# The last two output tiles of the second network's weights: prepared in the first chunk's expansion, from a staging pool

## The chip, the cores and the metric

One NeuronCore of a Trainium2 chip runs the whole program; the other cores are idle. The metric is the device time of one execution in microseconds (us). The engines are called PE (TensorE, matmuls), PEld (its weight loads), ACT (ScalarE), DVE (VectorE), POOL (GpSimd) and SP (SyncE, which here issues nearly all DMAs). Each engine works through its own list of instructions in a fixed order; an instruction that waits holds all that stand behind it on its engine.

## What is computed

Attention over 2304 tokens of width 512 (4 batches, 8 heads), then two feed-forward networks, one behind the other, all in float32:

```python
x = attention(q_l, k_l, v_l, q_g, k_g, v_g)            # 2304 x 512
g = x @ moe_w_gate                                     # first network, 512 -> 1536
x = (g * sigmoid(g) * (x @ moe_w_val)) @ moe_w_out     # 1536 -> 512
h = x @ moe2_w_in                                      # second network, 512 -> 2048
y = (max(h, 0) + alpha * min(h, 0)) @ moe2_w_out       # 2048 -> 512
```

The change touches only the weights `moe2_w_in` and `moe2_w_out` of the second network: when and from which memory they are prepared. What is computed stays the same.

## The kernel before

**Precision.** The weights arrive as 64-bit words. A float32 is taken out of each by ACT and DVE (`convert_steps`: ACT L765 and L766, DVE L768, L771, L777), and then split in a high and a low part (`split`: ACT copies the high half, L853, DVE subtracts for the low half in two pieces, L856). A product of two split operands is three matmuls. Blocks are multiplied by a scheme of Winograd's kind, seven products in place of eight, for which sums of weight blocks are wanted too: `block_sums` (L865) and `column_sums` (four DVE steps, L875).

**The second network's weights.** The generator `w2_prepare` does this for 16 tiles of 128 x 1024 words: for i = 0..3 the tiles ("x", 2i), ("x", 2i+1) of `w_in` and ("o", i), ("o", i+4) of `w_out`. A tile is loaded to a buffer `dbl` of 1 MB (L882), converted into `raw`, summed, split back into `dbl` and stored to DRAM (L890, 1 MB a store) as one of the arrays `w2sx`, `w2ss`, `w2so`, `w2st13`, `w2st42`. An "x" tile gives two stores, an "o" tile with j < 4 one, an "o" tile with j >= 4 three: its own, and with the tile j-4 the two sums t13 and t42. The `yield`s cut it into small steps, which the caller advances with `next(w2gen)` between its own instructions. The tile for the next item is loaded ahead.

**Stages.** Attention and two visits of the first network run under a planner; behind it (`nc.flush()`) comes the third visit of the first network, a loop over j = 0..5 of products (matmul L1278) and of the contraction `down3` (matmul L1335), in which `next(w2gen)` is called once or twice after each product and whose last turn, j = 5, begins by draining the generator. From there on the order on each engine is set when the program is built, by a list scheduler that goes by data dependences, buffers and the order of writing.

**The second network** runs over three chunks c of tokens. The expansion `up(c, jp)`, jp = 0..3, goes through seven products b11, t1, t2, b21, t3, b22, t4, each for jj = 0, 1, six matmuls each (L1483) into the banks ps_g and ps_v, ps_a, or ps_acc. ACT copies some partial sums out (L1514: `p` for b11 and t1, `u` for t2); t2 adds to the bank of b11 and t3 to that of t2. DVE adds the copies (L1508), ACT takes the two halves of the leaky relu (`hst`, L1500; `neg`, L1501) and DVE joins them (L1502) in `hst`. Then the contraction `down(c)` multiplies `hst` by `w_out` (also L1483, 256 columns). Its operands are tiles `as`, a ring of three, hi by ACT (L1581) and lo by DVE (L1582), after subtractions (L1561) for some products. The first two steps of the contraction are written inside jp = 3 already.

**Fetches.** `fetch_up` brings 1 MB for two products into one of four slots (four DMAs of 256 KB, L1253), `fetch_down` brings 1 MB of `w_out` weights into a ring of three (two DMAs, L1368); `down3` calls it for the first three at j = 3, 4, 5. All stand in SP's one list. The memory of `two` (the pool of `hst`, the temporary tiles and the `as` ring) is taken on the right side of SBUF before chunk 0 begins.

## Time and profile before

| | us |
|---|---|
| median of 3 runs | 870.16 (869.02 to 870.22) |
| profiled execution | 872.43 |
| its span in the trace | 870.6 |

The profile's page gives PE as busy for 850.0 us (98% of the span), PEld for 767.0, DVE for 655.3 and ACT for 568.8. The share of PE is above 0.9 in nearly all of the 40 slices. The span is what the trace covers; the execution's time lies 1.8 us above it. On the trace's clock the third visit of the first network runs from about 399 to 522 us, chunk 0's expansion from 522 to 586.4 (jp 1 begins at 542.7, jp 2 at 557.25, jp 3 at 571.8), and its contraction follows. A row's "idle before <-releaser" says how long the engine stood before the instruction, and what ended that.

### The profile page before, as it was taken

The numbers are of one execution on the slowest core, as the hardware profiler recorded it, in microseconds if no ns is written. First come the engines' busy times: TensorE is split into PE (matmuls) and PEld (weight loads), VectorE is DVE, ScalarE is ACT, GpSimd is POOL, SyncE is SP. The second block draws the span as 40 slices with busy tenths as digits, with TensorE's granted clock in tenths as the row PEclk, the third lists the DMA queues.
The fourth block names the chain that finished last, engine by engine and source line by source line (L and its number), as shares of the span: only waits on it lengthen the run. The fifth ranks groups of instructions, "written<-read, shape, count | busy, mean of one in ns | idle before, by whom it ended". The sixth has DMA issues, their size and how long they took to land.

```text
span 870.6 us, 18942 instructions
## 1 busy us (share of the span) xinstructions
PE 850.0 (98%) x7570; PEld 767.0 (88%) x7570; DVE 655.3 (75%) x1333; ACT 568.8 (65%) x1111; POOL 0.7 (0%) x6
## 2 busy tenths in 40 slices
PE   6899999999999999999999999999999999999997
PEld 5677778788788787888999999999999999999997
DVE  3987999988697665779989885589727699536863
ACT  4989999877567586655534446685437765357643
POOL 0000000000000000000000000000000000000000
PEclk9999999999999999999999999999999999999999
DMA  9799989899976869987898869887788887799497
GB/s 345 290 397 409 372 328 390 320 375 371 405 263 228 343 220 349 376 327 293 287 329 326 298 214 291 254 256 245 247 290 283 251 256 244 249 348 294 150 307 237
DMA packets 124312, 262.48 MB, mean 302 GB/s; under 512 B 7872, under 2 KB 96576, under 8 KB 109888
## 3 DMA queue, kind: packets, MB, share of 16 engines
q1 hardware_dynamic: 124224, 261.27, 85.0%
q8 instruction: 60, 0.98, 0.4%
q14 instruction: 28, 0.23, 0.1%
HBM read 198.06 MB, written 63.18 MB: 300 GB/s over the span
## 4 chain that ended last, share of the span: by engine, by line
PE 79%; ACT 7%; DVE 6%; DMA 5%; issue 2%; SPq 0%; ACTq 0%; DVEq 0%
PE ps_acc L1483 17%; PE ps_a L1483 10%; PE acc L274 9%; PE v L274 8%; PE g L274 8%; PE ps_g L1483 5%; PE a L274 5%; PE ps_v L1483 4%; PE ps_v L1278 3%; PE ps_g L1278 3%; PE ps_acc L1335 3%; PE ps_a L1335 2%; ACT e L274 2%; ACT L274 1%; DMA yp<-in_w_dram 1%
## 5 line engine op out<-in xcount | busy, mean ns | idle before, releaser
L1581 ACT ACTIVATE as<-hst 128x768 fp32r<-128x768 f32 (+2 forms) x100 | 70.3, 716 | 67.4 <-PE ps_acc L1483 41.8
L274 PE MATMUL g<-xa,w 128*128 128x512 f32 x432 | 107.7, 397 | 0.7 <-DVE xa L274 0.3
L1483 PE MATMUL ps_acc<-w,as 128*128 128x256 f32 x864 | 107.2, 282 | 0.7 <-DMA w<-w2st 0.4
L274 PE MATMUL v<-xa,w 128*128 128x512 f32 x432 | 107.1, 397 | 0.0
L274 PE MATMUL acc<-h,w 128*128 128x512 f32 x432 | 106.4, 395 | 0.5 <-DVE h L274 0.4
L1483 PEld LDWEIGHTS ps_acc<-w,as 128*128 128x128 f32 x864 | 104.6, 188 | 1.1 <-issue 0.5
L1582 DVE TENSOR_TENSOR as<-hst,as 128x768 fp32r<-128x768 f32 (+2 forms) x100 | 78.2, 793 | 34.4 <-ACT as L1581 34.0
L274 PEld LDWEIGHTS g<-xa,w 128*128 128x128 f32 x432 | 79.0, 188 | 20.5 <-issue 1.8
L274 PEld LDWEIGHTS acc<-h,w 128*128 128x128 f32 x432 | 79.7, 188 | 19.5 <-issue 1.4
L274 PEld LDWEIGHTS v<-xa,w 128*128 128x128 f32 x432 | 79.3, 188 | 18.4 <-issue 1.4
L274 ACT ACTIVATE e<-e,mx 128x128 f32<-128x128 f32 (+1 forms) x136 | 57.2, 423 | 19.3 <-DVE mx L274 18.9
L274 ACT ACT_TABLE_LOAD x42 | 53.9, 1283 | 10.3 <-PE g L274 8.9
L1502 DVE SCALAR_TENSOR_TENSOR hst<-neg,nal,hst 128x384 f32<-128x384 f32 (+1 forms) x96 | 56.5, 594 | 4.4 <-ACT neg L1501 2.6
L1483 PE MATMUL ps_a<-w,as 128*128 128x256 f32 x384 | 47.7, 281 | 0.0
L1483 PEld LDWEIGHTS ps_a<-w,as 128*128 128x128 f32 x384 | 46.5, 188 | 0.0
L1508 DVE TENSOR_TENSOR p<-ps_acc,p 128x384 f32<-128x384 f32 (+1 forms) x24 | 12.7, 531 | 43.6 <-PE ps_acc L1483 43.6
L274 DVE TENSOR_TENSOR t<-v,sg 128x512 f32<-128x512 f32 x36 | 24.7, 685 | 19.9 <-PE a L274 11.2
L1500 ACT ACTIVATE hst<-p 128x384 f32<-128x384 f32 (+1 forms) x48 | 24.3, 506 | 17.1 <-DVE p L1508 15.0
L274 PE MATMUL a<-qk 64*32 64x128 f32 (+1 forms) x1072 | 28.6, 294 | 5.4 <-DMA qk<-in_qk_dram 2.5
L1409 ACT ACTIVATE hring<-t 128x320 fp32r<-128x320 f32 x24 | 11.2, 467 | 32.3 <-DVE t L1408 32.3
L274 PEld LDWEIGHTS a<-qk 64*32 64x32 f32 x1072 | 18.9, 109 | 14.6 <-issue 4.0
L274 ACT ACTIVATE raw<-dbl 128x1024 f32<-128x1024 f32 x24 | 27.6, 1152 | 6.4 <-DMA w2ss<-raw 4.5
(265 smaller groups left out, 1740.8 us busy)
## 6 DMA issues: line engine op xcount, KB each, us to landing
dbl<-in_w_dram SPq DMA_DIRECT2D x28, 1024.0 KB, 8.6
w<-w2ss SPq DMA_DIRECT2D x96, 256.0 KB, 4.6
w<-w2st SPq DMA_DIRECT2D x48, 512.0 KB, 5.3
w<-w2so SPq DMA_DIRECT2D x40, 512.0 KB, 5.5
w<-w2sx SPq DMA_DIRECT2D x72, 256.0 KB, 4.7
v<-in_v_dram SPq DMA_DIRECT2D x15, 1024.0 KB, 9.8
qk<-in_qk_dram SPq DMA_DIRECT2D x14, 688.0 KB, 9.9
w2sx<-dbl SPq DMA_DIRECT2D x8, 1024.0 KB, 8.2
```

The costliest lines, as they stand in the source:

```text
L274: last[o.eng] = getattr(getattr(self.nc, o.eng), o.op)(*o.args, **o.kw)
L1278: nc.tensor.matmul(out=o[:, 0:n], lhsT=left(name, a, k), rhs=x[name][:, b, k, 0:n], start=(i == 0), stop=(i == 5),)
L1335: mm = nc.tensor.matmul(out=o, lhsT=a, rhs=x, start=(first and e == 0 and not second), stop=((j, f, e) == (NF1 // 2 - 1, 0, 2) and i not i ...
L1409: nc.scalar.activation(out=hi, in_=t, func=ACTF.Copy)
L1483: pe["last"] = nc.tensor.matmul(skip_group_check=True, **k)
L1500: nc.scalar.activation(out=h, in_=u, func=ACTF.Relu)
L1502: nc.vector.scalar_tensor_tensor(out=h, in0=g, scalar=nal[:, i:i + 1], in1=h, op0=ALU.mult, op1=ALU.add)
L1508: nc.vector.tensor_tensor(out=u, in0=o[:, 0:n], in1=u, op=ALU.add)
L1581: nc.scalar.activation(out=d[:, 0], in_=s, func=ACTF.Copy)
L1582: nc.vector.tensor_tensor(out=d[:, 1], in0=s, in1=d[:, 0], op=ALU.subtract)
```

## The change

`w2_prepare` is given the list of its tiles, the functions that give it buffers, and a number `pause`. The old generator does all but the last two tiles, ("o", 3) and ("o", 7). A second one, `w2rest`, does these two in chunk 0's expansion, from a pool `stage` on the right side: one `dbl` buffer of 8 KB per partition, and two `raw` buffers of 4 KB. With `pause` = 8 it waits eight calls before the conversion of each tile and before each of the two sums, and loads the second tile only after the first is stored. It is advanced once after each product and jj for jp < 3 and drained after the last product of jp = 2; then `stage` is released, and the operand ring `as` is allocated in its place as a pool `asp`, instead of in `two`. `fetch_down(1)` and `fetch_down(2)` move there too.

```diff
--- before.py
+++ after.py
@@ -875,7 +875,9 @@
             nc.vector.tensor_tensor(out=o, in0=x, in1=y, op=ALU.subtract)
             yield
 
-    def w2_prepare():
+    W2_ORDER = [(z, j) for i in range(NJ // 2) for z, j in (("x", 2 * i), ("x", 2 * i + 1), ("o", i), ("o", i + NJ // 2))]
+
+    def w2_prepare(todo, dbl_tile, raw_tile, pause):
 
         def land(z, j):
             dbl = dbl_tile()
@@ -897,13 +899,11 @@
             nc.sync.dma_start(out=w2s[key][:, 1], in_=raw)
             st["tail"] = False
 
-        todo = []
-        for j in range(NJ // 2):
-            todo += [("x", 2 * j), ("x", 2 * j + 1), ("o", j), ("o", j + NJ // 2)]
         dbl = land(*todo[0])
         for n, (z, j) in enumerate(todo):
-            ahead = land(*todo[n + 1]) if n + 1 < len(todo) else None
-            yield
+            ahead = land(*todo[n + 1]) if n + 1 < len(todo) and not pause else None
+            for _ in range(max(pause, 1)):
+                yield
             raw = raw_tile()
             yield from convert_steps(dbl, raw)
             yield
@@ -920,8 +920,10 @@
             else:
                 yield from column_sums(upper, raw)
                 for key, t in (("t13", upper), ("t42", raw)):
+                    for _ in range(pause):
+                        yield
                     yield from out_to((key, j - NJ // 2), t)
-            dbl = ahead
+            dbl = land(*todo[n + 1]) if pause and n + 1 < len(todo) else ahead
 
     def passes(a, b):
         return ((a[0], b[0]), (a[0], b[1]), (a[1], b[0]))
@@ -1101,7 +1103,7 @@
         att_tags["list"] = ["a0", "a1"]
         att_tags["i"] = 0
 
-        w2gen = w2_prepare()
+        w2gen = w2_prepare(W2_ORDER[:-2], dbl_tile, raw_tile, 0)
 
         def pumper(nslots, target, wrate=1.0, g=1.0):
             k0 = st["k"]
@@ -1344,7 +1346,8 @@
                 want_w1(2 * j + 6, "o")
                 wload(True)
             else:
-                fetch_down(j + 3 - NF1 // 2)
+                if j == 3:
+                    fetch_down(0)
 
         DOWN = (("b11", "b11"), ("s1", "t1"), ("s2", "t2"), ("a12", "b21"), ("s3", "t3"), ("s4", "b22"), ("a22", "t4"))
         HOME = {"b11": ("o", 0, 0), "b12": ("o", 0, 1), "b21": ("o", 4, 0), "b22": ("o", 4, 1),
@@ -1471,7 +1474,18 @@
 
             return hst[:, kt:kt + n, half(c) * q:half(c) * q + half(c)]
 
-        tags = {}
+        stage = tc.alloc_tile_pool(name="stage", bufs=1, side="right", reuse_waits="tile")
+        staged = {}
+
+        def stage_tile(size, dtype):
+            def new():
+                n = staged[size] = staged.get(size, 0) + 1
+                tag = "stage%d_%d" % (size, n % (1 if size == 2048 else 2))
+                return stage.tile([128, size * 4 // mybir.dt.size(dtype)], dtype, tag=tag, name="stage", bufs=1)
+
+            return new
+
+        w2rest = w2_prepare(W2_ORDER[-2:], stage_tile(2048, I64), stage_tile(1024, F32), 8)
 
         def temp(tag):
             return two.tile([128, 2, NT], F32, tag=tag, name=tag, bufs=1)
@@ -1567,7 +1581,7 @@
 
         def operand(c, what, kt):
 
-            t = two.tile([128, 2, 2, NT], F32R, tag="as%d" % (st["as"] % 3), name="as", bufs=1)
+            t = ring["as"].tile([128, 2, 2, NT], F32R, tag="as%d" % (st["as"] % 3), name="as", bufs=1)
             st["as"] += 1
             n = 256 if c == 2 else NT
             srcs = []
@@ -1735,6 +1749,15 @@
                     if jp == 3 and jj == 1 and name in ("b22", "t4"):
                         next(steps)()
                     tasks()
+                    if c == 0 and jp < NJ // 2 - 1:
+                        next(w2rest, None)
+                    if c == 0 and (jp, name, jj) == (NJ // 2 - 2, "t4", 1):
+                        for _ in w2rest:
+                            pass
+                        stage.release()
+                        ring["as"] = tc.alloc_tile_pool(name="asp", bufs=1, side="right", reuse_waits="tile")
+                        fetch_down(1)
+                        fetch_down(2)
             while late:
                 late.popleft()()
             extra.extendleft(reversed(list(s1_work(c, 3))))
@@ -1742,6 +1765,7 @@
                 pass
             while extra:
                 extra.popleft()()
+        ring["as"].release()
         two.release()
         slope.release()
         edge.release()
```

In the changed kernel the line numbers are shifted: L884 load and L892 store of the preparation, L1514, L1515, L1516 the relu (before L1500 to L1502), L1528 the copies (L1514), L1595 and L1596 the operand tiles (L1581, L1582).

The list scheduler moves instructions, in three places above all. The first is ACT around the end of jp 1 and the start of jp 2. In the kernel before (`hst` and `neg` are the relu's halves, `p` the copies that jp 2's first products leave):

```order
L1501 ACTIVATE neg<-p_6013 128x384 [waits Activation_49]
L1500 ACTIVATE hst<-u_6034 128x384 [waits DVE_49]
L1501 ACTIVATE neg<-u_6034 128x384 [waits Activation_49]
L1500 ACTIVATE hst<-u_6034 128x384 [waits DVE_49]
L1501 ACTIVATE neg<-u_6034 128x384 [waits Activation_49]
L1500 ACTIVATE hst<-ps_acc_5985 128x384 [waits PE_49]
L1501 ACTIVATE neg<-ps_acc_5985 128x384 [waits DVE_49]
L1500 ACTIVATE hst<-ps_acc_5998 128x384 [waits PE_49]
L1501 ACTIVATE neg<-ps_acc_5998 128x384 [waits DVE_49]
L1581 ACTIVATE as<-hst 128x768 [waits DVE_49]
L1514 ACTIVATE p_6144<-ps_g 128x384 [waits PE_49]
L1514 ACTIVATE p_6144<-ps_v 128x384 [waits PE_49]
```

The changed kernel at the same place:

```order
L1514 ACTIVATE hst<-p_5979 128x384 [waits DVE_49]
L1515 ACTIVATE neg<-p_5979 128x384 [waits Activation_49]
L1514 ACTIVATE hst<-u_6004 128x384 [waits DVE_49]
L765 ACTIVATE stage<-stage 128x1024 [waits DMAHW1_49]
L766 ACTIVATE stage<-stage 128x1024 [waits DMAHW4_49]
L1515 ACTIVATE neg<-u_6004 128x384 [waits Activation_49]
L1514 ACTIVATE hst<-u_6004 128x384 [waits DVE_49]
L1515 ACTIVATE neg<-u_6004 128x384 [waits Activation_49]
L1514 ACTIVATE hst<-ps_acc_5948 128x384 [waits PE_49]
L1515 ACTIVATE neg<-ps_acc_5948 128x384 [waits DVE_49]
L1528 ACTIVATE p_6120<-ps_g 128x384 [waits PE_49]
L1514 ACTIVATE hst<-ps_acc_5963 128x384
```

The two steps of tile ("o", 7)'s conversion stand between the halves of one relu, with a wait for its load; the operand tile is gone from here.

The second place is ACT where the expansion ends. Before, the list reads (two other `as` tiles stand earlier still, at the start of jp 1):

```order
L1500 ACTIVATE hst<-ps_acc_6294 128x384 [waits PE_49]
L1501 ACTIVATE neg<-ps_acc_6294 128x384 [waits DVE_49]
L1500 ACTIVATE hst<-ps_acc_6307 128x384 [waits PE_49]
L1501 ACTIVATE neg<-ps_acc_6307 128x384 [waits DVE_49]
L1031 ACTIVATE xa<-yp_94 128x2x128
L1581 ACTIVATE as<-hst 128x768 [waits PE_49] x3
```

In the changed kernel, where these are the first tiles `as` of all:

```order
L1514 ACTIVATE hst<-ps_acc_6301 128x384 [waits PE_49]
L1515 ACTIVATE neg<-ps_acc_6301 128x384 [waits DVE_49]
L1514 ACTIVATE hst<-ps_acc_6314 128x384 [waits PE_49]
L1515 ACTIVATE neg<-ps_acc_6314 128x384 [waits DVE_49]
L1595 ACTIVATE as<-hst 128x768 [waits DMAHW1_49]
L1595 ACTIVATE as<-hst 128x768 x2
```

All of the first three operand tiles have moved behind the last relu of jp 3, and the first waits for a DMA, the last store out of `stage`. Earlier in the same jp 3 ACT has the split for that store:

```order
L1514 ACTIVATE hst<-p_6308 128x384 [waits DVE_49]
L1515 ACTIVATE neg<-p_6308 128x384 [waits Activation_49]
L853 ACTIVATE stage<-stage 128x1024 [waits DMAHW3_49,Activation_49]
L1514 ACTIVATE hst<-p_6308 128x384 [waits DVE_49]
L1515 ACTIVATE neg<-p_6308 128x384 [waits Activation_49]
```

It stands between two relu pairs and waits for the store of t13 (`w2st_3` out of the same buffer). On SP the two last stores stand so, among the fetches for chunk 1 (`w2sx_165` and on; `DMAHW` and a number are the DMA queues' counters):

```order
L1255 DMA w<-w2sx_4890 128x2x256 [waits DMAHW2_49]
L892 DMA w2st_3_6281<-stage 128x2048 [waits DMAHW3_49,DVE_49,Activation_49]
L1371 DMA w<-w2so_5961 128x4x256 [waits DMAHW4_49]
L1255 DMA w<-w2sx_165 128x2x256 [waits DMAHW5_49,PE_49]
L1255 DMA w<-w2sx_170 128x2x256 [waits DMAHW6_49]
L1255 DMA w<-w2ss_166 128x2x256 [waits DMAHW7_49]
L1255 DMA w<-w2ss_171 128x2x256 [waits DMAHW0_49]
L892 DMA w2st_3_6286<-stage 128x2048 [waits DMAHW1_49,DVE_49,Activation_49]
L1255 DMA w<-w2ss_166 128x2x256 [waits DMAHW2_49,PE_49]
```

Where before only fetches stood:

```order
L1253 DMA w<-w2ss_4656 128x2x256 [waits DMAHW2_49,PE_49]
L1253 DMA w<-w2ss_5029 128x2x256 [waits DMAHW3_49]
L1253 DMA w<-w2sx_4495 128x2x256 [waits DMAHW4_49]
L1253 DMA w<-w2sx_4892 128x2x256 [waits DMAHW5_49]
L1253 DMA w<-w2sx_165 128x2x256 [waits DMAHW6_49,PE_49]
L1253 DMA w<-w2sx_170 128x2x256 [waits DMAHW7_49]
L1253 DMA w<-w2ss_166 128x2x256 [waits DMAHW0_49]
L1253 DMA w<-w2ss_171 128x2x256 [waits DMAHW1_49]
L1253 DMA w<-w2ss_166 128x2x256 [waits DMAHW2_49,PE_49]
```

The two stores are new in this place; each waits for ACT's and DVE's halves of its split, and the fetches behind it wait with it.

## Rows read from the trace of the kernel before

**Rows 1.** Windows: start:end length, busy us per engine (instructions), PE clock, DMA share, GB/s
```profile
424.00:446.00 22.00, 20.64 (x138) 20.22 (x137) 20.04 (x43) 12.26 (x20) 0.00 (x0) 1.00 0.89 305
446.00:500.00 54.00, 53.99 (x367) 53.64 (x366) 46.41 (x96) 23.21 (x40) 0.00 (x0) 1.00 0.89 324
500.00:522.20 22.20, 22.20 (x155) 21.91 (x154) 17.91 (x37) 10.38 (x20) 0.00 (x0) 1.00 0.66 208
522.20:542.70 20.50, 20.50 (x123) 20.13 (x123) 11.96 (x27) 11.75 (x33) 0.00 (x0) 1.00 0.93 293
...
571.80:586.40 14.60, 14.60 (x87) 14.60 (x86) 12.11 (x22) 11.19 (x27) 0.00 (x0) 1.00 0.84 260
```

**Rows 2.** Waits of PE from 424 to 586: us in total, times, longest
```profile
PE ps_v L1278 <- ACT p L1294: 1.4, 1, 1.4
```

**Rows 3.** Timeline of ACT at 441: start, us, instruction [idle before <-releaser]
```profile
441.06 2.01 ACT L853 ACTIVATE dbl<-raw 128x1024 fp32r<-128x1024 f32 x2 [2.39 <-DMA w2sx<-dbl]
```

**Rows 4.** Groups by form, 424 to 530: xcount, busy us, mean ns, idle before
```profile
L853 ACT ACTIVATE dbl<-raw 128x1024 fp32r<-128x1024 f32 x6 | 6.3, 1059 | 4.6 <-DMA w2sx<-dbl 2.4 <-DVE raw L777 1.3 <-DMA w2so<-dbl 0.9
L856 DVE TENSOR_TENSOR dbl<-raw,dbl 128x512 fp32r<-128x512 f32 x12 | 8.0, 685 | 0.9 <-ACT dbl L853 0.9
...
L766 ACT ACTIVATE dbl<-dbl 128x1024 int32<-128x1024 uint32 x2 | 2.3, 1140 | 0.0
L765 ACT ACTIVATE raw<-dbl 128x1024 f32<-128x1024 f32 x2 | 2.3, 1132 | 0.0
```

**Rows 5.** DMA issues of 1 MB and 0.25 MB, six windows: KB each, us to landing
```profile
dbl<-in_w_dram SPq DMA_DIRECT2D x1, 1024.0 KB, 8.2
...
w2sx<-dbl SPq DMA_DIRECT2D x1, 1024.0 KB, 8.7
...
w2so<-dbl SPq DMA_DIRECT2D x1, 1024.0 KB, 7.6
...
w2so<-dbl SPq DMA_DIRECT2D x1, 1024.0 KB, 6.6
...
w2st<-dbl SPq DMA_DIRECT2D x2, 1024.0 KB, 5.8
...
w<-w2ss SPq DMA_DIRECT2D x32, 256.0 KB, 4.6
```

**Rows 6.** Timeline of DVE at the first network's end
```profile
525.15 0.49 DVE L1410 TENSOR_TENSOR hring<-t,hring 128x320 fp32r<-128x320 f32 x1 [0.54 <-ACT hring L1409]
```

**Rows 7.** Timeline of PE, expansion of chunk 0 and start of its contraction
```profile
536.45 1.20 PE L1483 MATMUL ps_g<-w 128*128 128x384 f32 x6
...
561.41 1.20 PE L1483 MATMUL ps_g<-w 128*128 128x384 f32 x6
...
586.37 8.70 PE L1483 MATMUL ps_acc<-w,as 128*128 128x256 f32 x72
```

**Rows 8.** Timeline of ACT, the same stretch
```profile
543.08 0.49 ACT L1500 ACTIVATE hst<-ps_v 128x384 f32<-128x384 f32 x1
...
543.88 0.85 ACT L1581 ACTIVATE as<-hst 128x768 fp32r<-128x768 f32 x1
...
558.44 0.85 ACT L1581 ACTIVATE as<-hst 128x768 fp32r<-128x768 f32 x1
...
571.83 0.48 ACT L1501 ACTIVATE neg<-ps_g 128x384 f32<-128x384 f32 x1
...
581.25 0.51 ACT L1500 ACTIVATE hst<-p 128x384 f32<-128x384 f32 x1
...
587.80 0.50 ACT L1501 ACTIVATE neg<-ps_acc 128x384 f32<-128x384 f32 x1
...
588.70 0.85 ACT L1581 ACTIVATE as<-hst 128x768 fp32r<-128x768 f32 x1
```

**Rows 9.** Groups by form, 522 to 603, the two halves of an operand tile
```profile
L1582 DVE TENSOR_TENSOR as<-hst,as 128x768 fp32r<-128x768 f32 x9 | 8.6, 951 | 0.5 <-ACT as L1581 0.3
L1581 ACT ACTIVATE as<-hst 128x768 fp32r<-128x768 f32 x10 | 8.5, 847 | 5.4 <-PE ps_a L1483 2.7 <-PE ps_acc L1483 2.6
```

## The prediction

> **What bounds the kernel now.** The windows table comes first: it says for each stretch which engine is full. In the third visit of the first network TensorE computes 20.64 of 22.00 us, then 53.99 of 54.00, and in the last quarter (`jp` 3) of the expansion of chunk 0 14.60 of 14.60 [rows 1]. So TensorE's own work is the bound on both sides of the change, at the full granted clock (1.00). The DMA share is 0.89 in the first network and 0.93 and 0.84 in the first and last stretch of the expansion [rows 1]: the queues are no emptier where the work goes than where it comes from. The wait table is read next, for what could be won: from 424 to 586 us TensorE's only listed wait is 1.4 us for ACT's `p` copy [rows 2]. The ACT timeline gives its cause: the two splits of `dbl` (L853) began at 441.06 after 2.39 us of standing for a store `w2sx<-dbl` [rows 3], and `p` came behind them. That store took 8.7 us [rows 5].
>
> **Relief in the first network.** Two tiles leave: four ACT instructions of the conversion (2 x (1.13 + 1.14)) and four splits (4 x 1.06), 8.8 us in all, more than that on DVE, whose eight halves of the splits alone take 0.69 each [rows 4], and six transfers of 1 MB (two loads, four stores). All of it lay beside a full TensorE, so it is worth at most what TensorE idled. That is 1.4 us by the wait table. Its weight loads, which pause when a matmul starts late, idle 1.78, 0.36 and 0.29 us in the three stretches from 424 to 522 [rows 1], so 2.4 at the most and 0 at the least. The 1.4 us hangs on a store `w2sx`, and that tile (an "x" tile) is not among the two that leave. So I keep it, and take **-0.5 us** for the short ones.
>
> **Load and conversion in the expansion.** They add the same 8.8 us of ACT work to four `jp` of 14.55 us, in each of which ACT has about 3 us free (11.19 of 14.60 in the last [rows 1]). By sums it fits; by places it does not everywhere, because four of these instructions wait for a transfer at the head of an in-order queue. The price of 1 MB is the key number. Rows give 8.2 for a load and 8.7, 7.6, 6.6 and 5.8 for stores [rows 5]. I take 6.5 where fetches run beside it, and 5.8 to 8.7 as ends.
> Load 1: SP issues it when the last gated value of the first network is written, DVE's end at 525.15 + 0.49 = 525.64 [rows 6]. It lands at about 532.2. Behind its two ACT steps (2.27) stand two `p` copies and two `u` copies; TensorE needs the first `u` by `t3` at 536.45 [rows 7], so a landing up to about 533.2 is free. Term 0, at most 0.7.
> Load 2: the one `dbl` buffer of the stage must first be stored. The second half of o3's split stands on DVE beside the last multiply-adds of `jp` 0, whose ACT halves start at 543.08 [rows 8]. With one split ahead on ACT (1.06) and one half on DVE (0.69) the store leaves at 544.8, lands at 551.3, the load lands at 557.9. ACT waits for it ahead of the relu pairs at the end of `jp` 1; its two steps, five short ones and the copy `p<-ps_g`, on which `t2` adds, are some 4.5 us. They end at 562.4, and `t2` starts at 561.41 before [rows 7]: a stall of **1.0 us** (0 with 5.8, 5 with 8.7). SP stands at the same load until the store has landed. The slots behind it are fetched four ahead, and a slot lasts two of the seven names of a `jp`, 4.2 us of 14.6, so they are wanted over 10 us later, which covers it.
> Store of t13: ACT's split for it stands behind `neg<-ps_g` of `jp` 2, 571.83 before [rows 8], so with the shift of 1.0 it ends at 574.4; two DVE halves make it 575.8, the store leaves at about 576.2 and lands at 582.7.
>
> **The ring's gate.** This is the term that decides. Before, three operand tiles `as` were made long ahead: the first at 543.88, the third at 558.44 [rows 8]. When the expansion ends at 586.37, 72 contraction matmuls run on without a wait [rows 7], and ACT's next tile is made at 588.70 [rows 8], in time for the fourth. After, all tiles of the ring live in memory that the stage holds, so the order puts the first `as` behind the last relu pair of `jp` 3, with a wait for the last store, that of t42. Two chains lead there from the landing of t13's store at 582.7.
> By the store: split 1.06, two DVE halves 1.37, the store leaves at 585.1. Nothing but fetches for the next chunk stands ahead, so I take the row of the same kind, 5.8 (ends 4.9, a little over the 4.6 of a fetch of a quarter of the size, and 8.7 [rows 5]): it lands at 590.9, and `as` of 0.85 [rows 9] ends at 591.8.
> By ACT: behind that split stand the relu steps that ran from 581.25 to 588.30 before [rows 8], 7.0 us nearly without a gap. 583.8 + 7.0 + 0.85 = 591.7.
> Both give the first contraction matmul at about 591.8 instead of 586.4, so +5.4. These 5.4 contain the stalls above, since they are counted from the same starts. Two matmuls later the low half is wanted, DVE's 0.95 [rows 9], of which two matmuls hide 0.24: +0.7. After that ACT and DVE need 0.85 and twice 0.95 per 2.1 us of TensorE, and keep up. **Gate: +6.1 us**. The five transfers from o3's store to t42's stand in one chain, so their size counts five times: with 4.9 each no ACT step but the split itself comes later (580.8 + 1.06 + 7.0 + 0.85 = 589.7) and the gate is 4.1; with 7.5 each the same steps give load 2 at 559.8, o7's store at 576.5, t13's at 586.8, t42's at 596.8 and a gate of about 12; with 8.7 about 18. Waiting for its first operand TensorE has nothing else to run, and as it is full from there on nothing gives the loss back.
> The Trainium skill gives another price: DMA: Bandwidth & Descriptors, section "Anatomy of one DMA — SWDGE (gpsimd) path", fits a transfer as 2.0 us plus its bytes over 436 GB/s, an estimated 4.4 us for 1 MB. No 1 MB row here is that short, and these are issued by SP and share the queue with fetches [rows 5]. By it the stalls for load 2 and for t13's store vanish, ACT's chain alone stays, and the sum would be about +3.6, 873.8.
>
> **Sum.** -0.5 + 6.1 = +5.6 us. The profiled execution took 872.43 us, so 878.0; the median of the runs shown is 870.16, 2.27 less, so **875.8 us**. The measurement tells about 0.2% (1.7 us) from no change.
>
> **Rivals.**
> (a) Not slower: the gate is shorter and the relief whole. It needs transfers of about 4.9 us, so that no ACT step waits, and a last split that hides in ACT's gaps. Then ACT is through its relu pairs at 588.3, the first `as` ends at 589.1, +2.8 (and the low half is partly hidden); against it -1.4 to -2.4. That gives +0.4 to +1.4, 870.6 to 871.6. For it: ACT has 3 us free in each `jp`. Against: no 1 MB row below 5.8 [rows 5], and the 1.4 us hangs on a tile that stays.
> (b) Faster: the first network gains more than its visible waits, because 6 MB leave its DMA queues, and the ring's tiles are made as early as before. The Trainium skill speaks for this side: Perfetto Trace Analysis, section "Optimization Strategy", says that stretches with different most-contended engines may gain from being interleaved. Here TensorE is the full engine in both [rows 1], so I give it little. It would be -1.4 to -2.4, the idle time of the weight loads: 867.8 to 868.8 (below 868.4 it is told from no change).
> (c) Much slower: the expansion's queues are as full as the first network's (0.93 and 0.84), and the transfers take 7.1 us and more. Then load 2 holds ACT for 2 us and more at the end of `jp` 1, and by the chain above the gate is between 9 and 14, 879 to 884. For it: 8.7 and 8.2 in the rows. Against: the store rows fall to 5.8 toward the end of the first network, and jp 3 moves only 260 GB/s [rows 1].
>
> **How the numbers follow.** Forecast (872 to 879) 0.60; (a) 0.10; (b) 0.05; (c) 0.25. The range leaves out most of (b), part of (a) and the far end of (c): 871.0 to 883.0. Slower takes the forecast and (c): 0.85; same is (a): 0.10; faster is (b): 0.05.
>
> **What would show it.** The waits of TensorE after must list the contraction's `ps_acc` for ACT's `as` with about 5 us, once, and for DVE's `as` with 0.7, in chunk 0 alone. On ACT the first `as` must follow the last relu pair of `jp` 3, released by the store of t42 or without any idle time. The 1.4 us for `p` near 443 must still be there. A smaller wait of about 1 us must stand at `t2` of `jp` 2, put down to ACT `p`. The transfers of the stage must take 5.8 to 7 us each. I am wrong if the first contraction matmul waits under 2.5 us, if the wait near 443 is gone, or if a second kind of wait (TensorE for a fetch) appears in the expansion.

## The result, and the profile after

The changed kernel takes 877.76 us (median of 6 runs, 876.77 to 880.74) against 869.59 us before (6 runs): a ratio of 1.0099, 95% interval 1.0080 to 1.0117, some 8.2 us slower. A second series (e7, the changed kernel once more) gave 877.64 against 869.87 us, 1.0094 (1.0075 to 1.0113). The forecast was 875.8 us, 5.6 over before. The profiled execution took 877.2 us, its span is 875.3.

Two executions differ by some us in attention and the first two visits, whose instruction lists are the same in all kernels shown here: the third visit of the first network began at 405.4 us in the trace of before, at 402.1 in that of after, and between 400.6 and 403.3 in the others. So the traces are compared by pieces, from one first matmul to the next:

| us | third visit | expansion, chunk 0 | first 72 matmuls of its contraction | rest |
|---|---|---|---|---|
| before (three traces) | 116.89, 116.76, 117.18 | 64.12 in each | 8.54, 8.53, 8.53 | 275.2 to 276.2 |
| after (two traces) | 115.85, 115.46 | 70.42, 68.93 | 11.05, 12.16 | 275.9, 275.2 |

The third visit became about 1.3 us shorter, the expansion 4.8 to 6.3 longer, the start of the contraction 2.5 to 3.6 longer; behind it the traces of before and after lie in the same range. In the first trace of each this is -1.04 + 6.30 + 2.51 = +7.8 us, close to the medians' 8.2.

TensorE's waits, from 380 to 700 us of the trace after (us in total, times, longest); of before there was the one row [rows 2]:

```profile
PE ps_acc L1497 <- ACT as L1595: 3.7, 1, 3.7
PE ps_g L1497 <- ACT p L1528: 0.9, 1, 0.9
...
PE ps_acc L1497 <- DVE p L1522: 0.5, 1, 0.5
PE ps_acc L1497 <- DVE as L1596: 0.5, 1, 0.5
...
PE ps_g L1497 <- DVE p L1522: 0.2, 1, 0.2
```

One wait of 3.7 us for ACT's first operand tile, and 0.2 to 0.9 in four other places of the second network. The second trace of after, e7, has the same wait first:

```profile
PE ps_acc L1497 <- ACT as L1595: 3.6, 1, 3.6
```

Where the waits of the first trace stand, in the timeline of TensorE (start, duration, instruction, in brackets the idle time ahead and what ended it), against [rows 7]:

```profile
536.59 1.31 PE L1497 MATMUL ps_g<-xa,w 128*128 128x384 f32 x6 [0.20 <-DVE p L1522]
...
558.59 1.33 PE L1497 MATMUL ps_g<-w 128*128 128x384 f32 x6 [0.90 <-ACT p L1528]
...
583.41 1.31 PE L1497 MATMUL ps_acc<-xa,w 128*128 128x384 f32 x6 [0.49 <-DVE p L1522]
588.41 0.79 PE L1497 MATMUL ps_acc<-w,as 128*128 128x256 f32 x2 [3.69 <-ACT as L1595]
589.65 9.97 PE L1497 MATMUL ps_acc<-w,as 128*128 128x256 f32 x70 [0.45 <-DVE as L1596]
```

The first is `t4` of jp 0, the second `t2` of jp 2 (there the lag behind the kernel before, counted from the expansion's start, grows by 1.06 us, a little more than the idle time), the third the last six matmuls of the expansion. At 588.41 two contraction matmuls run, 0.45 us are lost on the low half, and then 70 matmuls take from 589.65 to 599.46, 9.81 us. In the trace of before 72 took 8.54, so 70 would be 8.30: 1.51 us go with no wait at all. The windows of the same stretch (length, busy us and instructions of PE, PEld, DVE, ACT, POOL, then granted clock, DMA share, GB/s) say why:

```profile
582.00:586.00 4.00, 2.23 (x12) 1.59 (x10) 4.00 (x9) 4.00 (x11) 0.00 (x0) 1.00 1.11 363
586.00:590.00 4.00, 1.14 (x3) 0.84 (x4) 4.00 (x7) 3.98 (x8) 0.00 (x0) 0.50 0.98 336
590.00:594.00 4.00, 4.00 (x24) 4.00 (x24) 3.08 (x4) 1.61 (x3) 0.00 (x0) 0.65 1.10 351
594.00:598.00 4.00, 4.00 (x36) 4.00 (x35) 3.55 (x4) 1.42 (x3) 0.00 (x0) 1.00 0.40 128
```

The granted clock is 0.50 from 586 to 590, a mean of 0.65 from 590 to 594, then 1.00. A mean of 0.65 over 4 us is 2.8 us at 0.50, the lower of the two levels (1.2 GHz): from 588.41 on TensorE ran some 4.4 us at half its rate, after it had idled 3.7 us. Before, the clock stood at 1.00 in every stretch [rows 1]. The coarser windows, of which [rows 1] has the first two and the fourth of before:

```profile
424.00:446.00 22.00, 21.39 (x140) 20.67 (x139) 20.21 (x44) 7.91 (x16) 0.00 (x0) 1.00 0.77 264
446.00:500.00 54.00, 54.00 (x373) 54.00 (x372) 36.49 (x76) 18.75 (x35) 0.00 (x0) 1.00 0.65 226
...
557.25:571.80 14.55, 13.65 (x78) 13.19 (x77) 14.05 (x26) 11.80 (x27) 0.00 (x0) 1.00 0.98 322
571.80:586.40 14.60, 12.43 (x71) 11.79 (x69) 12.06 (x23) 12.33 (x29) 0.00 (x0) 0.99 0.91 293
```

From 424 to 446 (on each trace's own clock; the third visit began 3.2 us earlier in the trace after) TensorE is busy 21.39 us in place of 20.64, its weight loads idle 1.33 in place of 1.78, and from 446 to 500 none at all in place of 0.36. In the windows from 557 and from 572 us it stands 0.90 and 2.17 us, where it was full, with a DMA share of 0.98 and 0.91 (before 0.79 and 0.84).

ACT's timeline shows the two chains that the forecast had drawn to the first operand tile, which in [rows 8] was made at 543.88:

```profile
554.00 1.12 ACT L765 ACTIVATE stage<-stage 128x1024 f32<-128x1024 f32 x1 [2.35 <-DMA stage<-in_w_dram]
...
579.44 1.06 ACT L853 ACTIVATE stage<-stage 128x1024 fp32r<-128x1024 f32 x1 [1.20 <-DMA w2st<-stage]
...
587.00 0.49 ACT L1515 ACTIVATE neg<-ps_acc 128x384 f32<-128x384 f32 x1
587.52 2.31 ACT L1595 ACTIVATE as<-hst 128x768 fp32r<-128x768 f32 x3
```

ACT stands 2.35 us for load 2 at the end of jp 1, and 1.20 us for t13's store in jp 3. The last relu half ends at 587.49, the first `as` begins at 587.52, with no idle time. The last store was issued at 581.89; its landing, and those of all six transfers of the stage in groups (KB each, us to landing), against [rows 5]:

```profile
w2st<-stage SPq DMA_DIRECT2D x1, 1024.0 KB, 5.6
```

```profile
stage<-in_w_dram SPq DMA_DIRECT2D x2, 1024.0 KB, 7.3
w2so<-stage SPq DMA_DIRECT2D x2, 1024.0 KB, 5.1
w2st<-stage SPq DMA_DIRECT2D x2, 1024.0 KB, 5.3
```

581.89 + 5.6 = 587.49: the store lands in the moment at which ACT is through. Either chain alone would have given this start. In e7 it is the same within 0.1 us: the store lands at 585.04, ACT is through at 585.11.

### The profile page after: what moved, and what is told of

Same layout as the page of the kernel before. It is cut to its first block, busy times and chain, and to the rows that moved or that the text cites. A ratio compares the mean times of both kernels' runs of the same rounds, so it can differ in the third digit from the quotient of the medians.

```text
span 875.3 us, 18948 instructions
## 1 busy us (share of the span) xinstructions
PE 852.3 (97%) x7570; PEld 768.2 (88%) x7570; DVE 656.1 (75%) x1333; ACT 567.2 (65%) x1111; POOL 0.7 (0%) x6
## 4 chain that ended last, share of the span: by engine, by line
PE 78%; DVE 9%; DMA 8%; ACT 3%; issue 1%; SPq 0%; ACTq 0%; DVEq 0%
PE ps_acc L1497 15%; PE acc L274 11%; PE g L274 10%; PE v L274 10%; PE ps_a L1497 8%; PE a L274 7%; PE ps_g L1497 4%; PE ps_v L1280 3%; PE ps_g L1280 3%; PE ps_v L1497 3%; PE ps_acc L1337 2%; DMA stage<-in_w_dram 2%; DVE hst L1516 2%; PE ps_a L1337 1%; DMA qk<-in_qk_dram 1%
## 5 line engine op out<-in xcount | busy, mean ns | idle before, releaser
L1595 ACT ACTIVATE as<-hst 128x768 fp32r<-128x768 f32 (+2 forms) x100 | 70.1, 716 | 70.7 <-PE ps_acc L1497 44.3
L1497 PE MATMUL ps_acc<-w,as 128*128 128x256 f32 x864 | 109.4, 285 | 4.8 <-ACT as L1595 3.7
L1596 DVE TENSOR_TENSOR as<-hst,as 128x768 fp32r<-128x768 f32 (+2 forms) x100 | 78.2, 794 | 34.8 <-ACT as L1595 34.5
L1516 DVE SCALAR_TENSOR_TENSOR hst<-neg,nal,hst 128x384 f32<-128x384 f32 (+1 forms) x96 | 56.1, 593 | 3.0 <-ACT neg L1515 1.6
L1514 ACT ACTIVATE hst<-p 128x384 f32<-128x384 f32 (+1 forms) x48 | 24.3, 505 | 16.2 <-DVE p L1522 13.8
L274 ACT ACTIVATE sg<-g 128x512 f32<-128x512 f32 x36 | 21.6, 601 | 15.3 <-PE g L274 15.0
L274 DVE CUSTOM_DVE_ANT_0 e<-a,lm 128x128 f32<-128x128 f32 x104 | 22.9, 285 | 11.3 <-PE a L274 11.2
```

Of the source, the lines that this page charges most:

```text
L274: last[o.eng] = getattr(getattr(self.nc, o.eng), o.op)(*o.args, **o.kw)
L1497: pe["last"] = nc.tensor.matmul(skip_group_check=True, **k)
L1514: nc.scalar.activation(out=h, in_=u, func=ACTF.Relu)
L1516: nc.vector.scalar_tensor_tensor(out=h, in0=g, scalar=nal[:, i:i + 1], in1=h, op0=ALU.mult, op1=ALU.add)
L1595: nc.scalar.activation(out=d[:, 0], in_=s, func=ACTF.Copy)
L1596: nc.vector.tensor_tensor(out=d[:, 1], in0=s, in1=d[:, 0], op=ALU.subtract)
```

## The experiments

Ratios are to runs of the kernel before on the same chip, with 95% intervals; pieces are those of the table above.

| run | median, us | before | ratio | third visit | expansion | first 72 |
|---|---|---|---|---|---|---|
| e1_two_left_out | 868.00 | 870.73 | 0.9964 (0.9947 to 0.9981) | 115.50 | 64.11 | 8.54 |
| e2_late_ring | 876.05 | 870.73 | 1.0058 (1.0035 to 1.0082) | 115.95 | 66.81 | 11.13 |
| e3_fill_wait | 876.52 | 870.73 | 1.0061 (1.0038 to 1.0083) | 115.49 | 68.96 | 9.78 |
| e4_pause2 | 873.74 | 870.73 | 1.0038 (1.0023 to 1.0052) | 115.54 | 70.05 | 9.26 |
| e5_two_buffers | 871.02 | 869.87 | 1.0018 (1.0004 to 1.0032) | 115.43 | 66.78 | 9.91 |
| e6_in_hst | 868.82 | 869.87 | 0.9994 (0.9982 to 1.0006) | 115.83 | 64.89 | 8.53 |
| e7_after_again | 877.64 | 869.87 | 1.0094 (1.0075 to 1.0113) | 115.46 | 68.93 | 12.16 |
| e8_in_hst4 | 868.40 | 871.11 | 0.9980 (0.9962 to 0.9998) | 115.64 | 64.11 | 8.54 |
| e9_in_hst5 | 869.38 | 871.11 | 0.9985 (0.9966 to 1.0003) | 115.47 | 64.11 | 8.54 |

e7 is the changed kernel itself, run beside e5 and e6. It was expected 7 to 9 us over before, with a wait of 3 to 4 us for ACT's first operand tile and the clock at 0.50 for some 4 us behind it. It came out 7.8 over, with a wait of 3.6; from the end of that wait the clock stood at 0.50 for longer, 6.8 us.

### What the first network gives back: e1, and two more traces of before

e1, on the kernel before:

```diff
+        todo = todo[:-2]
...
+                for kind, at in (("o", 3), ("o", 7), ("t13", 3), ("t42", 3)):
+                    w2s[kind, at] = w2s[kind, at - 1]
```

> The kernel before with the preparation of the last two output tiles left out altogether (the arrays of the tiles before them are read in their place, so the result is not the reference's); ring and fetches as before. It prices the relief of the first network alone. My theory (TensorE is full there, and only a few gaps hang on these two tiles): about 1.0 us less than before, as the traces of before and after put it between the first matmul of the third visit and the first of the expansion (116.9 against 115.9 us), no wait of 1.4 us near 443. Rival (the 6 MB less free the queues): 2.4 us less or more. Rival (the difference between the two traces is chance): 0 +- 0.3. In all cases the contraction of chunk 0 starts without a wait.

Measured: 0.36% less (0.19 to 0.53), 1.7 to 4.6 us. That leaves out the 1.0 us of my theory and takes in the rival's 2.4 and more. In its trace, though, the third visit takes 115.50 us, 1.4 less than in the traces of before, and TensorE's longest wait there is 0.3 us; expansion and contraction are those of before. The traces account for 1.4 us of the gain, nearer to the theory; the rest would lie in the part ahead, whose lists are the same, and it is open whether it is chance.

Whether the wait near 443 belongs to the kernel was then asked of two more executions of before, unaltered.

> The kernel before, unaltered, for a second trace of it. If the wait of 1.4 us near 443 and the late start of the third visit (405.4 us) in the first trace were chance: no wait over 0.5 us there, 115.4 to 116.0 us from the third visit's first matmul to the expansion's, and its start at 400 to 404 us. If they belong to the kernel: 1.4 us again, 116.5 to 117 us, and 405 us.

> The kernel before, unaltered, for a third trace of it, with the same two expectations: chance (no wait over 0.5 us near 443, 115.4 to 116.0 us from the third visit to the expansion, start of the third visit at 400 to 404 us) or kernel (1.4 us, 116.5 to 117 us, 405 us).

They had the third visit at 116.76 and 117.18 us, so its length belongs to the kernel. (Their third visits began at 403.05 and 402.79, so the 405.4 of the first trace was chance.) The wait near 443 does not come every time: e11 has it, with 1.35 us, but in e10 the same matmuls start at 441.23 with 0.11 us of idle time, and TensorE waits 0.94 us for another `p`, at 480.25. So neither expectation holds as a whole.

Both places have to do with the two tiles that leave. The first hangs on a row that I had misread. [rows 3] has "x2": two splits one behind the other. Only the first waited for the store `w2sx`; the second is o3's, one of the two tiles that leave. In the trace after ACT has one:

```profile
436.97 1.06 ACT L853 ACTIVATE dbl<-raw 128x1024 fp32r<-128x1024 f32 x1 [1.51 <-DMA w2sx<-dbl]
...
438.30 1.04 ACT L853 ACTIVATE w<-hring 128x1024 fp32r<-128x1024 f32 x1
```

One split of 1.06, then `hring`, then the weights' split; ACT is through at 439.34 and TensorE waits 0.1 us for the `p` behind it. Of the run e2, whose first network is that of before, the same place:

```profile
436.68 2.01 ACT L853 ACTIVATE dbl<-raw 128x1024 fp32r<-128x1024 f32 x2 [1.21 <-DMA w2sx<-dbl]
...
438.95 1.05 ACT L853 ACTIVATE w<-hring 128x1024 fp32r<-128x1024 f32 x1
439.90 0.41 ACT L1294 ACTIVATE p<-ps_v 128x320 f32<-128x320 f32 x1
```

Two splits again, but the store had landed 1.2 us earlier than in [rows 3] (an idle time of 1.21 against 2.39 us), and `p` came just in time, 0.16 us late: 115.95 us. In the four traces with two splits the wait is there in the two with a late store (2.39 and 2.40 us of idle time) and not in the two with an early one (1.16 and 1.21). Without o3's split no trace has a late store (1.1 to 1.5), so it is not shown that a late store alone would do no harm. The second place, in e10:

```profile
441.23 1.15 PE L1278 MATMUL ps_v<-xa,w 128*128 128x320 f32 x6
...
477.52 1.06 ACT L853 ACTIVATE dbl<-raw 128x1024 fp32r<-128x1024 f32 x1 [1.82 <-DMA w2so<-dbl]
...
480.25 1.11 PE L1278 MATMUL ps_g<-w,w 128*128 128x320 f32 x6 [0.94 <-ACT p L1294]
```

That split is t13's, behind o7's store `w2so`, which took 7.5 us here and 6.6 to 6.8 in the other three traces with this first network; all of it leaves with the two tiles. Over all traces the third visit takes 116.7 us in the mean of the four with the tiles (e2 among them) and 115.6 in the mean of the nine without, a relief of 1.1 to 1.3 us.

### The order alone: e2

On the kernel before, ACT's first three operand copies of chunk 0 are queued behind the last `neg`:

```diff
+                st["neg"] = nc.scalar.activation(out=g, in_=u, func=ACTF.Relu, scale=-1.0)
...
+                with tc.issue_after(st["neg"].ins) if c == 0 and st["as"] <= 3 else nullcontext():
+                    nc.scalar.activation(out=d[:, 0], in_=s, func=ACTF.Copy)
...
+                    if c and jp == 3 and jj == 1 and name in ("b22", "t4"):
+                        next(steps)()
...
+            if c == 0:
+                next(steps)()
+                next(steps)()
```

> The kernel before, with one thing added: ACT makes the first three operand tiles of chunk 0 behind the last relu of jp 3, as in the changed kernel, with no stage, no moved preparation and no store. My theory (the loss is the late single start of the contraction, and most of it is ACT's order): TensorE waits 2.7 to 2.9 us for the first tile and about 0.5 for its low half, then runs some us at a lower clock: 3.2 to 4.7 us more than before. Rival (the stage's transfers make the loss, the order alone is harmless): under 1 us more.

Measured: 0.58% more (0.35 to 0.82), 5.1 us, a little over the 3.2 to 4.7 expected, in the trace +2.69 in the expansion and +2.59 behind it. No byte and no instruction is added or moved out of the first network, and the lists of PE and SP are those of before; three ACT copies and their low halves come late. The timeline of TensorE and the windows:

```profile
584.89 0.51 PE L1483 MATMUL ps_acc<-w,as 128*128 128x256 f32 x2 [2.54 <-ACT as L1582]
586.10 10.09 PE L1483 MATMUL ps_acc<-w,as 128*128 128x256 f32 x70 [0.70 <-DVE as L1583]
```

```profile
584.00:588.00 4.00, 2.41 (x11) 2.20 (x12) 4.00 (x7) 2.60 (x5) 0.00 (x0) 0.78 0.77 251
588.00:592.00 4.00, 4.00 (x30) 4.00 (x29) 2.83 (x4) 0.90 (x2) 0.00 (x0) 0.79 0.00 0
```

2.54 us for the high half, 0.70 for the low half, and 9.92 us for 70 matmuls at a clock that fell to 0.78 in one window and 0.79 in the next. So more than half of the loss of the changed kernel comes with the order alone, and the clock adds to it: of the 5.3 us in the trace 2.7 lie at the high half, 1.0 at the low half and 1.6 in the 70 matmuls behind them.

### The clock: e3

```diff
+                if n == 0 and c == 0:
+                    for _ in range(30):
+                        matmul(out=o[0][:, 0:256], lhsT=w[:, 0, 0, 0:128], rhs=w[:, 0, 0], start=True, stop=True)
```

on the changed kernel, ahead of the first contraction matmul.

> The changed kernel with 30 matmuls added, whose sums are overwritten, between the last matmul of chunk 0's expansion and the first of its contraction, where TensorE waits 3.7 us: 30 x 0.12 = 3.6 us. They do no needed work and keep TensorE busy. My theory (the 1.5 us by which the 70 matmuls behind the wait are drawn out come from the granted clock, which fell to 0.50 after the idle time): the clock stays at 1.00, the 70 matmuls take 8.3 to 8.6 us instead of 9.8, and the time is 1.2 to 1.6 us under the changed kernel's, 6.6 to 7.0 over before. Rival (they are drawn out because operand tiles come late): no difference to the changed kernel, 8.2 over before.

```profile
582.44 3.75 PE L1497 MATMUL ps_acc<-w 128*128 128x256 f32 x30
586.16 0.50 PE L1497 MATMUL ps_acc<-w,as 128*128 128x256 f32 x2
587.53 8.57 PE L1497 MATMUL ps_acc<-w,as 128*128 128x256 f32 x70 [0.87 <-DVE as L1596]
```

```profile
584.00:588.00 4.00, 3.13 (x25) 2.75 (x24) 4.00 (x7) 4.00 (x8) 0.00 (x0) 1.00 1.00 346
588.00:592.00 4.00, 4.00 (x36) 4.00 (x35) 4.00 (x6) 1.58 (x4) 0.00 (x0) 1.00 1.10 352
```

The 30 matmuls fill 582.44 to 586.16, the clock stays at 1.00, and the 70 matmuls take 8.57 us in place of 9.97 (and 11.01 in the second trace of after). The late operand tiles are not what draws them out: the same tiles come as late here. The time is 0.61% over before (0.38 to 0.83) where the changed kernel had 0.94 and 0.99: the gain is 2.9 to 3.3 us at the point estimates, over the 1.2 to 1.6 expected, with intervals that still overlap a little. By the traces e3 is best held against e7, which like it has no wait at `t2` of jp 2: third visit and expansion are equal (115.49 and 115.46, 68.96 and 68.93), and the piece behind is 2.4 us shorter (9.78 against 12.16). The rest of the gain no trace places.

### The place of the last store: e4, e5

e4 is the changed kernel with `8` made `2` in the call of `w2_prepare`.

> The changed kernel with a pause of 2 in place of 8: the same work, the same stage, the ring in the same place, but the last store leaves some 9 us earlier, so that the order has the first operand tiles ahead of the last relus of jp 3. My theory (the start of the contraction is the loss): no wait over 1 us at the contraction, no fall of the clock there; the stall at t2 of jp 2 stays or grows to 1 to 2.5 us; 0.5 to 2.5 us over before. Rival (crowding of ACT and of the queues in the expansion is the loss, wherever the last store stands): the same 24 us of ACT, DVE and queue work in less time, 5 us over before or more.

Measured: 0.38% more (0.23 to 0.52), 3.3 us; both theories were partly wrong. The wait for the first operand tile is gone (0.5 for one low half is left), and so is the fall of the clock there. But in the profiled execution (875.87 us, by its pieces more over before than the median says) TensorE stands 2.64 us inside `t1` of jp 2:

```profile
561.14 1.33 PE L1497 MATMUL ps_a<-op,w 128*128 128x384 f32 x6 [2.64 <-DVE u L1522]
562.31 1.96 PE L1497 MATMUL ps_g<-w 128*128 128x384 f32 x6
564.06 2.05 PE L1497 MATMUL ps_v<-w 128*128 128x384 f32 x6
```

and the clock falls behind that wait too (six matmuls in 1.96 and 2.05 in place of 1.20). What it waits for is a DVE step, `u<-ps_a,u` at 560.54, which empties the bank. DVE's timeline ahead of it:

```profile
558.21 1.28 DVE L856 TENSOR_TENSOR stage<-stage 128x512 fp32r<-128x512 f32 x2
...
559.94 0.68 DVE L875 TENSOR_TENSOR stage<-stage 128x512 f32<-128x512 f32 x1
560.54 0.55 DVE L1522 TENSOR_TENSOR u<-ps_a,u 128x384 f32<-128x384 f32 x1
```

With a pause of 2 the scheduler puts o7's split (L856) and a column sum (L875), which follow on load 2, in front of an addition that TensorE waits for. Load 2 landed at 551.88, and from the first conversion step behind it DVE had no gap until that addition was through (the length, then the busy times of PE, PEld and DVE):

```profile
553.06:561.70 8.64, 6.00 (x35) 5.68 (x34) 8.64 (x16) 7.38 (x16) 0.00 (x0) 1.00 1.06 361
```

So in this stretch it is as the rival has it: the tile's work, packed close, crowds DVE's in-order list. e8 below shows that the same work, spread further, does not.

e5 is the changed kernel, pause 8, without the link between t13's store and t42's split:

```diff
+                    if pause:
+                        d = dbl.bitcast(F32R).rearrange("p (h c) -> p h c", h=2)[:, 0 if key == "t13" else 1]
...
+                        nc.scalar.activation(out=d, in_=t, func=ACTF.Copy)
...
+                                out=t[:, p0:p1].bitcast(F32R), in0=t[:, p0:p1], in1=d[:, p0:p1], op=ALU.subtract
...
+                        nc.sync.dma_start(out=w2s[k2][:, 0], in_=d.bitcast(F32))
+                        nc.sync.dma_start(out=w2s[k2][:, 1], in_=t)
```

> The changed kernel (pause 8, ring in the stage's place) with one link of its chain taken out: the splits of t13 and t42 write their high halves into different halves of the buffer and their low halves in place, so that t42 no longer waits for t13's store; each store becomes two of 0.5 MB. Its order has the first operand tiles ahead of the last two relu pairs of jp 3. My theory (the gate at the contraction is 6.6 of the 8.8 us, with the fall of the clock): no wait over 1 us at the contraction, the clock at 1.00 there; what stays is load 2 (1 to 1.3 us at t2 of jp 2) and 0.4 in jp 0: 1 to 2.5 us over before. Rival (the expansion is simply too full, as the 2.6 us stall of the run with a pause of 2 may say): a stall of 2 us or more shows up elsewhere, 4 us over before or more.

Measured: 0.18% more (0.04 to 0.32), 0.3 to 2.8 us, and 1.2 by the medians, in place of 7.8 in the same rounds. It is what my theory expected. (The profiled execution, 872.73 us, is 1.7 over its own median; its pieces are +2.7 in the expansion and +1.4 behind it.) The waits of TensorE over 0.3 us and ACT's first operand tile:

```profile
PE ps_acc L1510 <- DVE as L1609: 0.9, 1, 0.9
PE ps_g L1510 <- ACT u L1541: 0.8, 1, 0.8
PE ps_g L1510 <- DVE p L1535: 0.4, 1, 0.4
```

```profile
583.49 0.83 ACT L1608 ACTIVATE as<-hst 128x768 fp32r<-128x768 f32 x1
```

The tile is made at 583.49, ahead of the last two relu pairs, and TensorE goes from the expansion into the contraction at 585.45 without a wait; 0.9 us for one low half are left. From there on the clock is 1.00. Taking out one link of 5 us from a chain of five transfers, with the new order that the scheduler then found, was worth 6.6 us of the kernel's time.

### The moved work without the ring: e6, e8, e9

Here the buffers of the two tiles are rows of `hst` that jp 2 and jp 3 fill later, both loads are issued at the start, and the ring stays in `two`; e6 has a pause of 2, e8 of 4, e9 of 5.

```diff
-        stage = tc.alloc_tile_pool(name="stage", bufs=1, side="right", reuse_waits="tile")
...
+        spare8 = hst[:, 8:12].rearrange("p k n -> p (k n)")
+        spare12 = hst[:, 12:16].rearrange("p k n -> p (k n)")
+        stage_dbl = iter((spare8[:, 0:2048].bitcast(I64), spare12[:, 0:2048].bitcast(I64)))
+        stage_raw = iter((spare8[:, 2048:3072], spare12[:, 2048:3072]))
...
-            t = ring["as"].tile([128, 2, 2, NT], F32R, tag="as%d" % (st["as"] % 3), name="as", bufs=1)
+            t = two.tile([128, 2, 2, NT], F32R, tag="as%d" % (st["as"] % 3), name="as", bufs=1)
```

> The same two tiles prepared in chunk 0's expansion with a pause of 2, but from buffers inside hst (rows of jp 2 and jp 3, which are free until then), both loads issued at the start; the operand ring stays in the pool of before, made early as before. It does all the moved work and has neither the ring's gate nor load 2's wait for a store. My theory (the work as such hides beside TensorE): the contraction starts without a wait; stalls of 0.5 to 1.5 us in jp 0, where two conversions now stand, and none over 1 us later; -0.5 to 1.5 us against before. Rival (crowding of ACT, DVE and the queues costs by itself): 3 us over before or more.

> The run in hst's buffers with a pause of 4 in place of 2, so that the split of t13, which waited for a store ahead of the copies that t2 of jp 2 needs (0.5 us of wait there), stands behind them. My theory (what is left of the expansion's loss, 0.8 us, is this one place): no wait of TensorE in the expansion, 1.0 to 2.0 us under before, which is the whole relief of the first network. Rival (the work has its price wherever it stands): as with a pause of 2, within 1 us of before.

> The same with a pause of 5: the second tile's conversion stands one relu pair later as well, t13's split next to the first relu pair of jp 2. My theory: as with 4, 1.0 to 2.0 us under before, unless the first relu of jp 2, which now waits for o3's buffer and for t13's place, is late: then a wait of up to 1 us at jp 2 and no difference to before. Rival: as with a pause of 2.

e6: 0.9994 (0.9982 to 1.0006), no difference to before that could be told. The stalls that I had expected in jp 0 did not come. TensorE's waits in its trace, from 385 to 700 us:

```profile
PE ps_g L1280 <- DVE c L1288: 0.5, 1, 0.5
PE ps_g L1490 <- ACT p L1521: 0.5, 1, 0.5
PE ps_v L1280 <- DVE u L1304: 0.3, 1, 0.3
```

One wait of 0.5 us in the expansion, at `t2` of jp 2. With a pause of 4 it is gone, and the expansion takes 64.11 us with all the work in it:

```profile
PE ps_v L1280 <- DVE u L1304: 0.3, 1, 0.3
PE ps_g L1280 <- DVE c L1288: 0.2, 1, 0.2
```

e8 gives 0.9980 (0.9962 to 0.9998), e9 0.9985 (0.9966 to 1.0003). By the traces both have the whole relief, 1.3 and 1.5 us against the three traces of before, and no loss; by the times e8 lies below before by an interval that barely leaves out no change, and e9 by one that does not. So both are clearly faster than the changed kernel; that they beat the kernel before, by the little that the traces show, is likely and not more.

## Why the prediction was right, and where its sizes were off

**The direction and the place.** The forecast said that the contraction would start once, in chunk 0, about 5 us late, and it did: +6.30 us by the table, of which 3.9 at the first operand tile (in e7 +4.81, of which 3.8). That nothing gives the loss back was right too: the rest of the kernel takes the same time to within a us.

**The gate.** Predicted +5.4 with the stalls inside it; measured +6.3 and +4.8 in two executions. In the first the five transfers of the chain took 5.4 (o3's store), 7.6 (load 2), 4.8, 4.9 and 5.6 (the last three stores), 28.3 us against the 31.8 of the sum. (The lowest row of 1 MB, the 5.8 of [rows 5], stands for two stores, of 6.5 and 5.1 us in the trace of before; the second is near what the stage's stores took.) What was won there was not passed on, because t13's split has a fixed place on ACT, behind `neg<-ps_g` of jp 2: its store left at 574.42, 56.4 us behind the expansion's start, where the sum had 54.0, later by the stalls ahead of it and by the steps that DVE had in front of its halves. So that 5.4 lies between the two measurements is in part luck: transfers priced too high and stalls left out made up for each other. Both chains ended at nearly the same time, as their working said (591.8 and 591.7 on the clock of before). The +2.8 that rival (a) worked out for ACT's chain alone, with nothing late ahead of it, is what e2 shows: 2.69. e5 shows the other half: with the link taken out the scheduler no longer has to put the tiles last.

**The low half.** Predicted 0.7; 0.45 of wait in the trace after, where the first two matmuls ran at half the clock (from the first to the third 1.24 us, 1.0 more than the 0.24 of before); 0.70 in e2.

**The missing term: the clock.** The sum had every matmul behind the wait at its old duration. The 70 matmuls took 1.5 us more in one trace, 2.5 in the other, 1.6 in e2, and 0.1 with the wait filled (e3). This is the step of the sum that failed: "as it is full from there on nothing gives the loss back" is true, but the full TensorE first ran at half its rate, for 4.4 us in the first trace. With +1.5 to 2.5 the forecast would have been 877.3 to 878.3.

**The stalls on the way.** `t2` of jp 2 for ACT's `p`: predicted 1.0, measured 0.90 in one trace and none in the other, in which load 2 took 6.3 us in place of 7.6. `t4` of jp 0, which the sum did not have, lost 0.4 and 0.7: it waits for a DVE addition behind the conversion. The term for load 1 at `t3` of jp 0 (nothing, at most 0.7) was right for the two traces, in which that load took 6.9 and 7.3 us; where it took 7.9 and 8.2 (e4, e5), `t3` waited 0.5 and 0.8. The last six matmuls of the expansion waited 0.5 for `p<-ps_acc` at 582.80, behind the DVE halves of t42's split (in e7 they did not wait); the sum had left that out.

**The relief.** Predicted -0.5, measured -1.1 to -1.3. The step that failed is "the 1.4 us hangs on a store `w2sx`, and that tile (an "x" tile) is not among the two that leave": the row had two splits, and the second was o3's. The wait near 443 was to stay and is gone, one of the three signs by which the prediction called itself wrong; as before has it in two of four traces only, its absence alone would have told little. Nor did the stage's transfers keep to the 5.8 to 7 us that were to show it (4.8 to 7.6). The wait at the first operand tile, the order on ACT and the stall at `t2` of jp 2 came as announced, the last in one of two traces.

**The rivals.** (a) and (b) fell with the gate; (b)'s gain is the relief, which the traces of e1, e8 and e9 keep because the ring is left where it was. (c) priced the transfers too high. The moved work as such costs nothing when it is spread: e8 has all of it, at no loss in the expansion; packed close, in e4, it cost a wait of 2.6 us at one place, and the clock behind it. The estimate of 4.4 us by the Trainium skill (DMA: Bandwidth & Descriptors, section "Anatomy of one DMA — SWDGE (gpsimd) path") is below all twelve transfers of the two traces, which took 4.8 to 7.6 us; for the stores it is near, for the loads it is not, and its sum, 873.8, is 4 us short of the result.

The net, with the first trace of after: -1.3 + 6.3 + 2.5 = +7.5, against -0.5 + 6.1. The relief was bigger by 0.8, the start of the contraction dearer by 2.7, nearly all of it the clock and the small stalls.

## What to carry to other kernels

When a buffer takes over the memory of another, its first use waits for the last reader of the old one, and here the list scheduler put it behind everything that was ready: look at what the new owner used to do early. Price a wait of the full engine with the clock behind it, not with its own length alone. Where a row of a timeline says "x2", ask what each of the two is before saying whose wait it is, and take a second trace before calling one wait a part of the kernel.

## What the runs showed of the hardware

After idle times of 2.5 us (e2, with a further 0.7 behind two matmuls), 2.6 us (e4) and 3.6 to 3.7 us (the two traces of after) the granted clock fell to 0.50 and TensorE lost a further 1.5 to 2.5 us; after 2.0 us (before, at 51 us), 1.4 us (before, near 443) and 0.9 us (after, jp 2) the windows show 1.00. The length of one wait does not settle it: from 26 to 30 us TensorE is busy 1.96 of 4 us in e4 and 1.97 in the trace after, at the same place of the kernel, and from 30 to 34 us the clock is 0.57 in the one and 1.00 in the other. The Trainium skill (TensorE: Matmul & The Clock Gate, section "What's actually happening") describes the clock as a gate with two states that goes by recent activity; the rows agree, and e3 shows that matmuls without use hold it open. A store of 1 MB out of the stage took 4.8 to 6.3 us in a stretch with a DMA share above 0.9, and a load of 1 MB 6.3 to 7.6.
